# Attention in a pre-LN block: two row maxima per vector instruction, one ring of banks, a new order of steps

## The chip, the core and the metric

The kernel runs on one core of a Trainium2 chip. The metric is the device time of one execution in microseconds (us). Engines are called by the profile's names: PE (matmul), PEld (weight load), DVE (VectorE), ACT (ScalarE), POOL (GpSimd) and SP (the engine that issues most DMAs). "L228" is line 228 of the kernel.

## The reference

One block with 2048 tokens of width 512: layer norm, attention with 32 heads of 16, a residual; then layer norm and a gated MLP, and a second residual.

```python
def _A_ref(x, wqkv, wo):
    B, S, D = x.shape            # 1, 2048, 512
    H = 32; Dh = D // H          # 16
    qkv = (x @ wqkv).reshape(B, S, 3, H, Dh).transpose(2, 0, 3, 1, 4)
    q, k, v = qkv[0], qkv[1], qkv[2]
    scores = jnp.einsum("bhqd,bhkd->bhqk", q, k) * Dh ** -0.5
    p = _softmax(scores, axis=-1)
    o = jnp.einsum("bhqk,bhkd->bhqd", p, v)
    return o.transpose(0, 2, 1, 3).reshape(B, S, D) @ wo

h = x + _A_ref(_layernorm(x), wqkv, wo)
h2 = h + _B_ref(_layernorm(h), w_in, w_sp, b_sp, w_out)   # the gated MLP, not touched here
```

The softmax subtracts a maximum of each row of scores. So the kernel needs, for each head and query, a maximum over the 2048 keys before it can take exponentials.

## The kernel before

The kernel has three parts. First come layer norm and the projections to q, k and v, then attention, then the output projection and the MLP. The change is in attention, whose instruction order is written out by hand for all engines: an engine runs its instructions in the order of the program, and tiles bring the waits between engines.

**Units and pairs.** Heads are taken four at a time (`hg`, 8 groups) and queries 512 at a time (`qb`, 4 blocks). Such a block has 16 key blocks of 128 keys. One key block is a unit, and the loop at L1045 takes two units, a pair: 256 pairs, eight in each block. Two heads (`p`) times two row halves of PE (`t`) make a group's four heads: `t` = 0 uses PE rows from 0, `t` = 1 rows from 64, so that two matmuls with 48 or 50 rows each can stand in the array side by side.

**A pair's scores.** `score` (L808) makes one 128 x 512 tile of scores in PSUM, in a bank of its own, by one matmul (`product`, L805), and ACT takes its exponential into `pt` (L814). The steps are named s0 to s7: s0 to s3 belong to the first key block, s4 to s7 to the second; odd ones have `t` = 1.

**Weighing.** `weigh` (L825) multiplies the exponentials with the values into one bank `pv`, with four column groups of PE (L830). In the order it is "P" for the pair's first key block (the whole width, 512 queries), and "H", twice, for the second key block of the pair before (256 queries each). "P" needs s0 to s3, "H" needs s4 to s7 of the pair before. At the end of a block "out" (`take`, L840) copies `pv` out on DVE and sends it to memory. The next block's "P" reuses the bank and waits for that copy.

**A pair's maxima.** Beside its scores each pair does a part of the row maxima for a later block (`max_pair`, L205): for 128 queries and two heads. With `t` = 1 it takes four maxima over 512 keys each (M0, M4, M5, M7). With `t` = 0 it takes two such (M1, M2), and for the other 1024 keys a pair of tiles: "minus" (M3, ACT takes the absolute value, L233) and "plus" (M6, a DVE instruction that combines the two, L237). A single maximum is one matmul (L223) and one DVE reduction of 128 x 512 to 128 x 1 (L228). After eight pairs one block's maxima are complete. Then `finish` ("join") reduces them to one number for each head and query (L242, DVE), and POOL scales it and splits it in two halves (L245, L246, L247). `max_rows` ("turn") transposes these on DVE (L259) and sends them over a scratch tensor into two extra rows of the query tile (L260, L263), where the score matmul adds them in. The set of maxima is made ahead: eleven pairs' worth (LEAD) is done before attention begins, so the last ten or so pairs have none.

**PSUM in attention.** There are eight banks. Scores have three in turn (`ps_s`), maxima four in turn (three of `ps_m` and `ps_m3`), and `pv` one. A matmul into a bank waits until the reader of that bank's former contents is done.

**The order.** The string PAIR (L40) gives the order of a pair's steps, and the loop at L1099 issues them:

```python
PAIR = "s0 M0 join s2 M4 M1 s1 H s3 invert M2 s5 M3 H out M5 s4 M7 turn s6 s7 M6 P".split()
```

"join" runs `finish` of the pair before, if it was the last of a block's eight. "invert" takes the reciprocal of a block's row sums (L777) in one pair of eight, after a DMA that has gathered them. POOL has other work beside, queued at the start of a pair by `work` (L1048): it scales and splits the weights of the later parts. In the pair that follows a block's last maxima no such work is queued. In the last ten pairs, which have no maxima, `scores2` (L816) makes two score tiles at a time.

Of the kernel before, what the change touches and what calls it, by code (L numbers as in the profile page):

```python
# [8 lines left out]
F32 = mybir.dt.float32  # L9
# [6 lines left out]
AX = mybir.AxisListType  # L16
PSUM = bass.MemoryType.PSUM
DRAM = bass.MemoryType.DRAM

P = 128  # L20
S = 2048
D = 512
H = 32
# [4 lines left out]
NB = S // P  # L28
# [4 lines left out]
KS = 48  # L33
# [3 lines left out]
FIRST = 2  # L37
RG = 64
VW = DH + 1
PAIR = "s0 M0 join s2 M4 M1 s1 H s3 invert M2 s5 M3 H out M5 s4 M7 turn s6 s7 M6 P".split()  # L40
HF = 3 * P
FC = FH // 2
LOW = -3.0e38
# [16 lines left out]
def block_kernel(ctx: ExitStack, tc: tile.TileContext, x, wqkv, wo, w_in, w_sp4, b_sp, w_out, out):  # L60
# [139 lines left out]
    def bank(i):  # L200
        if i in more:
            return more[i]()
        return ps_m.tile([P, 512], F32, name=f"m{i}")

    def max_pair(m):  # L205

        g, i = divmod(m, 8)
        hg, qb = divmod(g, NQ)
        q, k, w = qst[g], kst[hg % 2], uvs[hg % 2]
        if i == 0:
            mx[g] = sm.tile([P, 16, 4], F32, name="mx")
            nc.gpsimd.memset(mx[g][:, :8, 3:], LOW)
        c, p = slice(i % 4 * P, i % 4 * P + P), i // 4
        at = lambda t, e: mx[g][:, t * 8 + i, e:e + 1]

        def scores(t, keys, b):  # L220
            r = slice(RG * t, RG * t + KS)
            acc = bank(b)
            nc.tensor.matmul(acc, q[r, p, c], keys[r, p], start=True, stop=True)  # L223
            return acc

        def one(t, e, b):
            acc = scores(t, k[:, :, 512 * e:512 * e + 512], b)
            nc.vector.reduce_max(at(t, e if t else e - 1), acc, axis=AX.X)  # L228

        def minus(b):  # L230
            acc = scores(0, w[:, :, 512:], b)
            ab[0] = sm.tile([P, 512], F32, name="ab")
            nc.scalar.activation(ab[0], acc, AF.Abs)  # L233

        def plus(b):
            acc = scores(0, w[:, :, :512], b)
            nc.vector.tensor_tensor_reduce(ab[0], acc, ab[0], 0.5, LOW, ALU.add, ALU.max, at(0, 0))  # L237

        def finish():
            if i == 7:  # L240
                nm = sm.tile([P, 2, 8], F32, name="nm")
                nc.vector.tensor_reduce(nm.rearrange("p t i -> p (t i)"), mx.pop(g), axis=AX.X,  # L242
                                        op=ALU.max, negate=True)
                parts = sm.tile([P, 2, 2, 8], F16, name="mparts")
                nc.gpsimd.tensor_scalar(nm, nm, 1.0 / ONE, 1.0, op0=ALU.mult, op1=ALU.mult)  # L245
                nc.gpsimd.tensor_copy(parts[:, :, 0], nm)  # L246
                nc.gpsimd.tensor_sub(parts[:, :, 1], nm, parts[:, :, 0])  # L247
                turned[0] = (g, parts)

        ab = {}  # L250
        four = [lambda b, e=e: one(1, e, b) for e in range(4)]
        two = [lambda b, e=e: one(0, e, b) for e in (2, 3)]
        return [four[0], two[0], two[1], minus, four[1], four[2], plus, four[3], finish]

    def max_rows():

        g, parts = turned.pop(0)
        t = sm.tile([P, 32], F16, name="mturned")
        nc.vector.transpose(t, parts.rearrange("p t j i -> p (t j i)"))  # L259
        nc.sync.dma_start(m_scr[g % 2], t)  # L260
        for j in range(2):
            r0 = RG * j + KS
            nc.sync.dma_start(  # L263
                qst[g][r0:r0 + 2].rearrange("r p (c n s) -> r (p c) n s", n=4, s=32),
                m_scr[g % 2].rearrange("(n j r q) s -> j r q n s", n=4, j=2, r=2)[j])
# [476 lines left out]
    def make_h(sb, acc):  # L742

        o2, h = o2s.pop(sb), xrs[sb]
        for d in range(DB):
            for i, (a, b) in enumerate(((0, 0), (0, 1), (1, 0))):
                nc.tensor.matmul(acc, o2[a][:, d, :], wo2[b][:, d, :],
                                 start=not (d or i), stop=d == DB - 1 and i == 2)
                if d < DB - 1 or i < 2:
                    yield  # L750
        nc.vector.scalar_tensor_tensor(h, acc, h_down, h, op0=ALU.mult, op1=ALU.add)
        nc.sync.dma_start(h_scr[sb * P:(sb + 1) * P, :], h)
        hst[sb] = e2.tile([P, 6], F32, name="st")
        nc.vector.bn_stats(hst[sb], h)
# [18 lines left out]
    def invert():  # L773

        hg, cols, sums, pool = sums_.pop(0)
        rc = pool.tile([P, 16], F32, name="rcp")
        nc.vector.reciprocal(rc, sums)  # L777
        to = four_heads(r_scr.rearrange("(d h) s -> d h s", h=8), hg)[:, :, cols]
        for t in range(2):
            nc.sync.dma_start(to[t].rearrange("p (r c) -> p r c", c=16), rc[64 * t:64 * t + 64])  # L780
# [7 lines left out]
    with ExitStack() as at:  # L788
# [3 lines left out]
        fixed(kst[1])  # L792
        pp = at.enter_context(tc.tile_pool(name="pp", bufs=6))
        ps_v = at.enter_context(tc.tile_pool(name="ps_v", bufs=1, space=PSUM))
        inner = at.enter_context(ExitStack())
        ps_m3 = inner.enter_context(tc.tile_pool(name="ps_m3", bufs=1, space=PSUM))
        ps_s = inner.enter_context(tc.tile_pool(name="ps_s", bufs=3, space=PSUM))
        more.clear()
        more[3] = lambda: ps_m3.tile([P, 512], F32, name="m3")
        pv = {}  # L800

        def product(s, hg, qb, kb, p, t):
# [5 lines left out]
        def score(hg, qb, kb, p, t):  # L808

            if (p, kb) not in pts:  # L810
                pts[p, kb] = pp.tile([P, 2, 512], F32, name="pt")
            s = ps_s.tile([P, 512], F32, name="s")
            product(s, hg, qb, kb, p, t)
            nc.scalar.activation(pts[p, kb][:, t, :], s, AF.Exp, scale=scales_[hg // 2])  # L814

        def scores2(hg, qb, kb, p):  # L816

            pts[p, kb] = pp.tile([P, 2, 512], F32, name="pt")
            turn[0] += 1
            s = later[turn[0] % 3 != 1].tile([P, 2, 512], F32, name="s2")  # L820
            for t in range(2):
                product(s[:, t, :], hg, qb, kb, p, t)
            nc.scalar.activation(pts[p, kb], s, AF.Exp, scale=scales_[hg // 2])
# [221 lines left out]
        for n in range(0, len(units), 2):  # L1045
# [12 lines left out]
                copy_v()  # L1058
            if kb == 2 and n // NB + 3 < HG * NQ:
                load_q(n // NB + 3)  # L1060
            steps = max_pair(m) if m < 8 * HG * NQ else []
            m += 1
            if not steps and not later:
                maxima.close()
                later.append(attn.enter_context(
                    tc.tile_pool(name="ps_l", bufs=1, space=PSUM, side="right")))
                steps_h.append(make_h(h_rows[0], later[0].tile([P, 512], F32, name="h")))
            elif not steps and len(later) == 1:
                inner.close()
                later.append(at.enter_context(tc.tile_pool(name="ps_t", bufs=2, space=PSUM)))  # L1070
            ends = kb == 0 and n

            def join():
                if joins:
                    joins.pop()()
# [20 lines left out]
                some_h(1)  # L1096
                weigh(hg, qb, kb)
            first = True
            for tok in PAIR if len(later) < 2 else ():  # L1099
                i = int(tok[-1]) if tok[-1].isdigit() else 0  # L1100
                if tok[0] == "s":
                    score(hg, qb, (kb, kb1)[i // 4], i % 4 // 2, i % 2)
                elif tok[0] == "M" and steps:
                    steps[i](count[0] % 4)
                    count[0] += 1
                    if i == 6:
                        joins.append(steps[8])
                elif tok == "join":
                    join()
                elif tok == "H" and prev is None:  # L1110
                    if first:
                        pv[0] = ps_v.tile([P, 512], F32, name="pv")
                        for j in range(4):
                            nc.tensor.matmul(pv[0][32 * j:32 * j + 32, :], vst[0][:, :32],
                                             vst[0][:, :512], start=True, stop=True)
                    first = False
                elif tok == "H":
                    a = 0 if first else 256
                    weigh(*prev, a, a + 256)
                    first = False  # L1120
                elif tok == "P":
                    weigh(hg, qb, kb)
                elif tok == "out" and ends:
                    take(*prev[:2])
                elif tok == "invert" and kb == 6 and n > NB:
                    invert()
                elif tok == "turn" and turned:
                    max_rows()
            prev = (hg, qb, kb1)
            if len(later) == 2 and kb == 6:  # L1130
                invert()
# [472 lines left out]
```

## Time and profile before

| | |
|---|---|
| median of 3 runs | 1713.44 us (1712.44 to 1714.61) |
| span of the profiled execution | 1712.3 us, 36689 instructions |
| what lies around the span | 1.1 us, against the median |
| granted clock of PE | 1.00 in all stretches of attention |
| attention with maxima | about 161 to 1248 us |

The profiled execution is the one that the page and all answers of the trace are about. A row of a window gives, for each engine, its busy time and the count of its instructions. A row of a group gives the line, the engine, the tile written and the tiles read, the count, then after the bar the busy time and the mean duration in ns, and then the engine's idle time just before such instructions with what ended it. A row of the timeline gives the start in the span, the time to the end of the last instruction of the row, and then the instructions, merged where several of one line follow each other.

### The profile page before, as it was taken

How to read it: one execution, taken by the hardware profiler on the slowest of the kernel's cores; microseconds unless marked ns; L12 is line 12 of the kernel's file. 1: busy time of each engine (PE TensorE's matmuls, PEld its weight loads, DVE VectorE, ACT ScalarE, POOL GpSimd, SP SyncE). 2: the span in 40 equal slices, each digit the busy share in tenths (PEclk: the TensorE clock that was granted, in tenths of full speed). 3: DMA queues.
4: the chain of work that ended last, by engine and by line, in shares of the span. 5: the costliest groups of instructions: out<-in, count | busy, mean ns of one | idle time of the engine just before them, and what ended most of it. 6: DMA issues, size and time to landing. Idle time of an engine off the chain costs nothing.

```text
span 1712.3 us, 36689 instructions
## 1 busy us (share of the span) xinstructions
PE 1699.5 (99%) x13508; PEld 644.7 (38%) x13508; DVE 1452.5 (85%) x3051; ACT 1317.5 (77%) x2584; POOL 813.6 (48%) x1062
## 2 busy tenths in 40 slices
PE   9999999999999999999999999999999999999999
PEld 4533222222222222222222222222225666656665
DVE  7688999999999999999999999999936787543444
ACT  4334999999999999999999999999995545211111
POOL 1231867776673267687767776400002766300100
PEclk9999999999999999999999999999999999999999
DMA  5534332342221244344434444300114454664551
GB/s 185 167 94 144 103 89 68 101 94 82 81 68 25 56 118 117 104 144 125 130 113 124 132 140 130 80 13 19 37 39 124 140 173 140 233 234 156 198 217 44
DMA packets 189309, 196.03 MB, mean 114 GB/s; under 512 B 67496, under 2 KB 140008, under 8 KB 189128
## 3 DMA queue, kind: packets, MB, share of 16 engines
q1 hardware_dynamic: 186824, 188.04, 36.8%
q10 hardware_dynamic: 2304, 5.64, 0.8%
q8 instruction: 106, 1.74, 0.4%
q14 instruction: 75, 0.61, 0.1%
HBM read 122.10 MB, written 65.93 MB: 110 GB/s over the span
## 4 chain that ended last, share of the span: by engine, by line
PE 78%; DVE 12%; DMA 3%; POOL 2%; ACT 2%; SPq 2%; issue 1%; ACTq 0%; POOLq 0%; DVEq 0%
PE pv L830 26%; PE s L805 17%; PE m L223 9%; DVE mx L228 7%; PE acc L107 4%; PE g L108 4%; PE g L109 4%; PE g L107 4%; PE acc L109 4%; PE acc L108 4%; DMA rc<-r_scr 1%; DVE ab L237 1%; DVE og L840 1%; SPq L723 1%; DVE rs_t L124 1%
## 5 line engine op out<-in xcount | busy, mean ns | idle before, releaser
L814 ACT ACTIVATE pt<-s 128x512 f32<-128x512 f32 x1968 | 1006.2, 637 | 5.5 <-PE m L223 4.3
L228 DVE TENSOR_REDUCE mx<-m 128x1 f32<-128x512 f32 x1510 | 947.5, 682 | 11.7 <-PE m L223 2.9
L805 PE MATMUL s<-qst,kst 50*128 50x512 f16 x2048 | 604.2, 379 | 0.2
L830 PE MATMUL pv<-pt,vst 128*32 128x256 f32 (+1 forms) x6056 | 598.1, 466 | 4.1 <-DVE og L840 1.3
L223 PE MATMUL m<-kst,qst 48*128 48x512 f16 x1510 | 452.4, 381 | 0.0
L805 PEld LDWEIGHTS <-kst 50*128 50x128 f16 x2048 | 132.0, 94 | 352.1 <-issue 323.7
L830 PEld LDWEIGHTS pv<-pt,vst 128*32 128x32 f32 x6056 | 119.5, 108 | 290.7 <-issue 277.3
L223 PEld LDWEIGHTS <-qst 48*128 48x128 f16 x2048 | 159.2, 93 | 173.6 <-issue 124.2
L223 PE MATMUL m<-uvs,qst 48*128 48x512 f16 x504 | 190.5, 380 | 0.6 <-DVE mx L228 0.6
L245 POOL TENSOR_SCALAR nm<-nm 128x16 f32<-128x16 f32 x32 | 6.6, 206 | 358.8 <-DVE nm L242 358.8
L237 DVE CUSTOM_DVE_ANT_0 ab<-m,ab 128x512 f32<-128x512 f32 x252 | 170.5, 677 | 2.7 <-ACT ab L233 2.7
L233 ACT ACTIVATE ab<-m 128x512 f32<-128x512 f32 x252 | 157.3, 624 | 15.5 <-PE m L223 14.8
L1368 ACT ACTIVATE pr<-pr,up 128x304 f32<-128x304 f32 (+1 forms) x32 | 17.0, 574 | 109.2 <-DVE up L1322 109.2
L991 POOL TENSOR_TENSOR op<-raw,op 128x512 f16<-128x512 f32 x80 | 92.9, 1161 | 6.0
L914 POOL TENSOR_TENSOR raw<-raw 128x512 f32<-128x512 f32 (+1 forms) x84 | 83.3, 991 | 6.7
L919 POOL TENSOR_TENSOR acc_sp<-acc_sp,raw 128x512 f32<-128x512 f32 x63 | 80.4, 1277 | 4.5
L109 PE MATMUL acc<-wi,hT 128*128 128x344 f16 x256 | 79.1, 309 | 0.3 <-DVE hT L104 0.3
L107 PE MATMUL acc<-wi,hT 128*128 128x344 f16 x256 | 79.1, 309 | 0.0
L108 PE MATMUL acc<-wi,hT 128*128 128x344 f16 x256 | 79.1, 309 | 0.0
L1510 POOL TENSOR_TENSOR pr<-pr,z 128x344 f32<-128x344 f32 x8 | 7.3, 914 | 145.9 <-DMA whole<-squares 108.3
L911 POOL TENSOR_SCALAR raw<-raw 128x512 f32<-128x512 f32 (+1 forms) x88 | 52.3, 594 | 19.7 <-DMA raw<-in_wqkv 12.4
L1509 DVE TENSOR_TENSOR pr<-g,v 128x344 f32<-128x344 f32 x8 | 4.1, 517 | 66.6 <-PE g L109 63.5
(247 smaller groups left out, 2292.9 us busy)
## 6 DMA issues: line engine op xcount, KB each, us to landing
raw<-in_w_sp SPq DMA_DIRECT2D x128, 256.0 KB
s_scr<-op SPq DMA_DIRECT2D x64, 256.0 KB
op<-s_scr SPq DMA_DIRECT2D x32, 512.0 KB
a_scr<-op SPq DMA_DIRECT2D x48, 256.0 KB
op<-a_scr SPq DMA_DIRECT2D x24, 512.0 KB
o_scr<-og SPq DMA_DIRECT2D x64, 128.0 KB
qst<-q_scr SPq DMA_DIRECT2D x192, 32.0 KB
kst<-k_scr SPq DMA_DIRECT2D x48, 128.0 KB
```

The source lines that it names most:

```text
L107: nc.tensor.matmul(ps, lh, rh, start=first, stop=False, **kw)
L108: nc.tensor.matmul(ps, lh, rl, start=False, stop=False, **kw)
L109: nc.tensor.matmul(ps, ll, rh, start=False, stop=last, **kw)
L223: nc.tensor.matmul(acc, q[r, p, c], keys[r, p], start=True, stop=True)
L228: nc.vector.reduce_max(at(t, e if t else e - 1), acc, axis=AX.X)
L233: nc.scalar.activation(ab[0], acc, AF.Abs)
L237: nc.vector.tensor_tensor_reduce(ab[0], acc, ab[0], 0.5, LOW, ALU.add, ALU.max, at(0, 0))
L805: nc.tensor.matmul(s, kst[hg % 2][r, p, kb * P:(kb + 1) * P], qst[hg * NQ + qb][r, p, :], start=True, stop=True)
L814: nc.scalar.activation(pts[p, kb][:, t, :], s, AF.Exp, scale=scales_[hg // 2])
L830: nc.tensor.matmul(pv[0][32 * j:32 * j + 32, a:b], vst[hg % 2][:, c:c + 32], pts[j % 2, kb][:, j // 2, a:b], start=kb == 0, stop=kb == NB - 1,
L914: pool.tensor_mul(got[0] if n else acc, got[0], got[0])
L991: chores.append((lambda: pool.tensor_sub(t[0][:, 1], of(), t[0][:, 0]), TT))
```

## The change

Four of the six single maxima of a pair become two double ones. `both` writes two matmuls (one with `t` = 0, one with `t` = 1) into the two banks of a tile `dd`, and one DVE instruction reduces 128 x 2 x 512 to two columns of the maxima's tile. There is one such tile, so the second double of a pair waits for the first one's reduction. All other tiles of a pair (eight scores, two single maxima, minus and plus) take turns in one ring of five banks, whoever reads them. With `pv` that makes eight banks again.

The order of steps is new. In it "X" is a double maximum, "N" a single one, "A" is minus, "C" is plus, "Q" is what "H" was, "R" what "P" was, and "rows" stands for join and invert. The first pair of a block has an order of its own, with "out" and without "rows". `plus` now comes behind the whole product R, and "turn" two tokens behind "rows". In the pairs without maxima, the tile `dd` and four newly opened banks serve `scores2`, and the tile `h` for the output projection is made when the ring has closed.

```diff
-PAIR = "s0 M0 join s2 M4 M1 s1 H s3 invert M2 s5 M3 H out M5 s4 M7 turn s6 s7 M6 P".split()
+PAIR = "s1 X s3 s4 Q s0 N s2 s5 Q X A N s6 rows s7 turn R C".split()
+FIRST_PAIR = "s1 X s3 s4 Q N s0 s2 Q out s5 X A s7 s6 N turn R C".split()
+SINGLES = 5
...
+    class Banks:
+
+        def __init__(self, pools, double):
+            self.pools = [pool for pool, n in pools for _ in range(n)]
+            self.turn, self.double = 0, double
+
+        def one(self):
+            i = self.turn % len(self.pools)
+            self.turn += 1
+            return self.pools[i].tile([P, 512], F32, name=f"c{i}")
+
+        def two(self):
+            return self.double.tile([P, 2, 512], F32, name="dd")
...
-            acc = bank(b)
+            acc = banks.one() if banks else bank(b)
...
+        def both(e):
+            acc = banks.two()
+            for t in range(2):
+                keys = k[:, :, 512 * (e - 2 * t):512 * (e - 2 * t) + 512]
+                r = slice(RG * t, RG * t + KS)
+                nc.tensor.matmul(acc[:, t, :], q[r, p, c], keys[r, p], start=True, stop=True)
+            a = 4 * i + e - 1
+            nc.vector.reduce_max(mx[g].rearrange("p n e -> p (n e)")[:, a:a + 32:31], acc, axis=AX.X)
...
+        if banks:
+            wide = PAIR.count("X")
+            return {"N": four[wide:], "n": two[wide:], "A": [minus], "C": [plus], "end": finish,
+                    "X": [lambda e=e: both(e) for e in (2, 3)]}
...
+        maxima.close()
+        more.clear()
+        ps_d = at.enter_context(tc.tile_pool(name="ps_d", bufs=1, space=PSUM))
         inner = at.enter_context(ExitStack())
-        ps_m3 = inner.enter_context(tc.tile_pool(name="ps_m3", bufs=1, space=PSUM))
-        ps_s = inner.enter_context(tc.tile_pool(name="ps_s", bufs=3, space=PSUM))
-        more.clear()
-        more[3] = lambda: ps_m3.tile([P, 512], F32, name="m3")
+        ps_c = inner.enter_context(tc.tile_pool(name="ps_c", bufs=1, space=PSUM))
+        banks = Banks([(ps_c, SINGLES)], ps_d)
...
-            s = ps_s.tile([P, 512], F32, name="s")
+            s = banks.one()
...
-            s = later[turn[0] % 3 != 1].tile([P, 2, 512], F32, name="s2")
+            s = banks.two() if turn[0] % 3 == 1 and SINGLES == 5 else later[1].tile([P, 2, 512], F32, name="s2")
...
-            steps = max_pair(m) if m < 8 * HG * NQ else []
+            steps = max_pair(m, banks) if m < 8 * HG * NQ else []
             m += 1
             if not steps and not later:
-                maxima.close()
-                later.append(attn.enter_context(
-                    tc.tile_pool(name="ps_l", bufs=1, space=PSUM, side="right")))
-                steps_h.append(make_h(h_rows[0], later[0].tile([P, 512], F32, name="h")))
+                later.append(None)
             elif not steps and len(later) == 1:
                 inner.close()
+                later[0] = at.enter_context(tc.tile_pool(name="ps_l", bufs=1, space=PSUM))
                 later.append(at.enter_context(tc.tile_pool(name="ps_t", bufs=2, space=PSUM)))
+                steps_h.append(make_h(h_rows[0], later[0].tile([P, 512], F32, name="h")))
...
-            for tok in PAIR if len(later) < 2 else ():
+            for tok in (FIRST_PAIR if ends else PAIR) if len(later) < 2 else ():
...
+                elif tok in ("A", "C", "N", "n", "X"):
+                    if steps:
+                        steps[tok].pop(0)()
...
+                elif tok == "R":
                     weigh(hg, qb, kb)
-                elif tok == "out" and ends:
+                elif tok == "out":
                     take(*prev[:2])
-                elif tok == "invert" and kb == 6 and n > NB:
-                    invert()
+                elif tok == "rows":
+                    join()
+                    if kb == 6 and n > NB:
+                        invert()
                 elif tok == "turn" and turned:
                     max_rows()
+            if steps:
+                joins.append(steps["end"])
             prev = (hg, qb, kb1)
```

More of the change, by code (lines that the diff above doesn't have):

```diff
@@ L203, in bank, with max_pair @@
         return ps_m.tile([P, 512], F32, name=f"m{i}")
-    def max_pair(m):
+    class Banks:
[8 more added lines that the diff above has]
+            return self.double.tile([P, 2, 512], F32, name="dd")
+    def max_pair(m, banks=None):
         g, i = divmod(m, 8)
@@ L221, in scores, with one, minus @@
             r = slice(RG * t, RG * t + KS)
-            acc = bank(b)
+            acc = banks.one() if banks else bank(b)
             nc.tensor.matmul(acc, q[r, p, c], keys[r, p], start=True, stop=True)
             return acc
-        def one(t, e, b):
+        def one(t, e, b=None):
             acc = scores(t, k[:, :, 512 * e:512 * e + 512], b)
             nc.vector.reduce_max(at(t, e if t else e - 1), acc, axis=AX.X)
-        def minus(b):
+        def both(e):
[6 more added lines that the diff above has]
+            nc.vector.reduce_max(mx[g].rearrange("p n e -> p (n e)")[:, a:a + 32:31], acc, axis=AX.X)
+        def minus(b=None):
             acc = scores(0, w[:, :, 512:], b)
@@ L233, in minus, with plus @@
             nc.scalar.activation(ab[0], acc, AF.Abs)
-        def plus(b):
+        def plus(b=None):
             acc = scores(0, w[:, :, :512], b)
@@ L250, in max_pair @@
         ab = {}
-        four = [lambda b, e=e: one(1, e, b) for e in range(4)]
-        two = [lambda b, e=e: one(0, e, b) for e in (2, 3)]
+        four = [lambda b=None, e=e: one(1, e, b) for e in range(4)]
+        two = [lambda b=None, e=e: one(0, e, b) for e in (2, 3)]
+        if banks:
+            wide = PAIR.count("X")
+            return {"N": four[wide:], "n": two[wide:], "A": [minus], "C": [plus], "end": finish,
+                    "X": [lambda e=e: both(e) for e in (2, 3)]}
         return [four[0], two[0], two[1], minus, four[1], four[2], plus, four[3], finish]
@@ L1098, in block_kernel @@
             first = True
-            for tok in PAIR if len(later) < 2 else ():
-                i = int(tok[-1]) if tok[-1].isdigit() else 0
+            for tok in (FIRST_PAIR if ends else PAIR) if len(later) < 2 else ():
                 if tok[0] == "s":
+                    i = int(tok[1])
                     score(hg, qb, (kb, kb1)[i // 4], i % 4 // 2, i % 2)
[L1103 to L1110, printed above, removed]
+                elif tok in ("A", "C", "N", "n", "X"):
+                    if steps:
+                        steps[tok].pop(0)()
+                elif tok == "Q" and prev is None:
                     if first:
@@ L1116, in block_kernel @@
                     first = False
-                elif tok == "H":
+                elif tok == "Q":
                     a = 0 if first else 256
@@ L1120, in block_kernel @@
                     first = False
-                elif tok == "P":
+                elif tok == "R":
                     weigh(hg, qb, kb)
-                elif tok == "out" and ends:
+                elif tok == "out":
                     take(*prev[:2])
-                elif tok == "invert" and kb == 6 and n > NB:
-                    invert()
+                elif tok == "rows":
+                    join()
+                    if kb == 6 and n > NB:
+                        invert()
                 elif tok == "turn" and turned:
                     max_rows()
+            if steps:
+                joins.append(steps["end"])
             prev = (hg, qb, kb1)
```

## The prediction

> **What bounds the kernel now.** First the page's busy line, then the windows of a stretch of attention, then the groups of 200 to 1250 us.
>
> ```profile
> PE 1699.5 (99%) x13508; PEld 644.7 (38%) x13508; DVE 1452.5 (85%) x3051; ACT 1317.5 (77%) x2584; POOL 813.6 (48%) x1062
> 600.00:700.00 100.00, 99.66 (x904) 28.19 (x905) 99.25 (x194) 99.95 (x205) 72.66 (x104) 1.00 0.40 112
> L814 ACT ACTIVATE pt<-s 128x512 f32<-128x512 f32 x1892 | 967.5, 637 | 2.1 <-PE m L223 1.0
> L228 DVE TENSOR_REDUCE mx<-m 128x1 f32<-128x512 f32 x1418 | 888.9, 682 | 7.6
> ```
>
> In attention PE, DVE and ACT are all over 99% busy, so busy time can't say which of them sets the pace. The timelines can. Of ACT, with one L233 row in each pair of key blocks:
>
> ```profile
> 656.94 0.62 ACT L233 ACTIVATE ab<-m 128x512 f32<-128x512 f32 x1
> 661.35 0.62 ACT L233 ACTIVATE ab<-m 128x512 f32<-128x512 f32 x1
> 665.86 0.64 ACT L233 ACTIVATE ab<-m 128x512 f32<-128x512 f32 x1
> 670.36 0.64 ACT L233 ACTIVATE ab<-m 128x512 f32<-128x512 f32 x1
> 674.79 0.62 ACT L233 ACTIVATE ab<-m 128x512 f32<-128x512 f32 x1
> 675.27 4.06 ACT L814 ACTIVATE pt<-s 128x512 f32<-128x512 f32 x8
> 679.20 0.62 ACT L233 ACTIVATE ab<-m 128x512 f32<-128x512 f32 x1
> ```
>
> A plain pair lasts 4.41 us (674.79 to 679.20) and holds nine ACT instructions: 0.49 each. They overlap (0.62 long, the next one 0.48 later), and the eight end at 679.33, 0.49 before the end of the ninth (679.82): no gap. **ACT is saturated.** Now PE:
>
> ```profile
> 672.52 0.37 PE L805 MATMUL s<-qst,kst 50*128 50x512 f16 x1
> 672.82 0.64 PE L830 MATMUL pv<-pt,vst 128*32 128x256 f32 x8
> 673.39 0.39 PE L805 MATMUL s<-qst,kst 50*128 50x512 f16 x1
> 673.40 0.39 PE L223 MATMUL m<-kst,qst 48*128 48x512 f16 x1
> 673.62 0.38 PE L805 MATMUL s<-qst,kst 50*128 50x512 f16 x1
> 673.93 0.64 PE L830 MATMUL pv<-pt,vst 128*32 128x256 f32 x8
> 674.50 0.39 PE L223 MATMUL m<-kst,qst 48*128 48x512 f16 x1
> 674.73 0.38 PE L223 MATMUL m<-kst,qst 48*128 48x512 f16 x1
> 675.29 1.06 PE L830 MATMUL pv<-pt,vst 128*32 128x512 f32 x8
> 676.29 0.39 PE L805 MATMUL s<-qst,kst 50*128 50x512 f16 x1
> ```
>
> A score and a maximum on opposite row halves start together (673.39, 673.40): one slot of 0.23 us. From the last slot of a group to a product it is 0.30 (672.52 to 672.82, 673.62 to 673.93); a half product takes 0.57, a whole one 1.00. Eight slots in groups of three, two and three with their products need 5 x 0.23 + 3 x 0.30 + 2 x 0.57 + 1.00 = 4.19. DVE:
>
> ```profile
> 699.79 3.07 DVE L228 TENSOR_REDUCE mx<-m 128x1 f32<-128x512 f32 x5
> L1357 DVE TENSOR_REDUCE low<-pr 128x2 f32<-128x768 f32 x7 | 6.7, 953 | 0.7
> ```
>
> Five reductions of 0.68 in 3.07 make one per (3.07 - 0.68) / 4 = 0.60, so seven vector steps are 4.2 in a pair. So PE and DVE have about 0.2 us of slack per pair and ACT has none. Between 200 and 1250 us, 1892 exponentials and 237 absolutes at 0.49 make 1043 of the 1050 us. Only 7 us are not ACT's own.
>
> **What the change does, part by part.** *ACT*: eight exponentials and one absolute per pair as before, so 4.41 stays the floor, and whatever DVE saves is not on the path. At most those 7 us and their like can come back.
>
> *Double maxima.* From the rows 768 columns cost 0.953 and 512 cost 0.682: 1.06 ns a column. A reduction over 1024 then lasts 0.682 + 0.54 = 1.22, and one follows after 0.60 + 0.54 = 1.14. Two of them save 4 x 0.60 - 2 x 1.14 = 0.12 us per pair on DVE, under ACT's cover. The end that saves nothing (1.20) leaves DVE at its old load, so the pair is still 4.41; there is no end at which the saving shows.
>
> The Trainium skill, "VectorE: DVE Perf Modes", section "The DRAIN you can't avoid", has the next instruction start only when the pipe is empty, and its rules for kernel authors say to minimise the number of operations. By that, two singles would be 1.36 and a double 1.22, 0.28 saved per pair. The trace has the next reduction start 0.08 before the former's end, so the measurement decides; the full saving is a rival below.
>
> *The ring of five and the new order.* PE now runs [C of the pair before, s1, X, s3, s4] Q [s0 N s2 s5] Q [X A N s6 s7] R: again eight slots, 4.19. But a step now waits for the bank used five single steps earlier, whichever engine reads it. The remaining durations:
>
> ```profile
> 748.22 0.39 PE L805 MATMUL s<-qst,kst 50*128 50x512 f16 x1
> 748.65 2.56 ACT L814 ACTIVATE pt<-s 128x512 f32<-128x512 f32 x5 [0.78 <-PE m L223]
> L814 ACT ACTIVATE pt<-s x1968: 591/645/680, 160.7 to 1253.5; 128x512 f32<-128x512 f32 x197
> 661.30 0.68 DVE L840 COPY og<-pv 128x512 f32<-128x512 f32 x1
> 662.04 1.06 PE L830 MATMUL pv<-pt,vst 128*32 128x512 f32 x8
> ```
>
> From a matmul's start its reader starts 0.43 later (748.22 to 748.65), and an exponential ends 1.02 after it (0.43 + 0.59). A reader's end frees PE 0.05 later (661.98 to 662.04). Put 0 at the end of s1's exponential. With ACT saturated the others end at s3 0.49, s4 0.98, s0 1.47, s2 1.96, s5 2.45, A 2.94, s6 3.43, s7 3.92, next s1 4.41. Each matmul must start 1.02 before its end.
>
> - s2 takes s1's bank (from 0.05), s5 takes s3's (0.54), A s4's, N s0's, s7 s2's (2.01), C s5's, the next s1 A's.
> - s5 starts at 0.54, Q at 0.84, X at 1.41, A and N at 1.64, s6 at 1.85, s7 at 2.01, R at 2.31. C and the next s1 start at 3.31 and end at 4.33: **0.08 early**.
> - then X at 3.54 and s3, s4 at 3.76; Q at 4.06 and s0 at 4.63, ending 5.65 against 5.88.
> - DVE, in the same clock: C 3.74, X 4.34, N 5.48, the next X at 6.25 (it waits for PE), N 7.39 to 8.07. That N frees the following s3, whose matmul must start by 8.29: 0.17 early.
>
> So a plain pair should stay at 4.41, at small margins.
>
> *First pair of a block.* Before, DVE's copy og holds R: R started at 662.04 instead of 0.30 after its last slot, and the ACT rows above show 4.51, 4.50 and 4.43 for three pairs: 0.21 us lost per block. In the new order og starts on DVE at 1.66, ends 2.34, and R starts at 2.39 instead of 2.31: inside the 0.08. The loss should go: 30 blocks x 0.21 = 6.3 us. Its other end is nothing gained.
>
> *`rows` and `turn`.* Once per eight pairs `rows` issues L242 on DVE, POOL makes three small steps, and `turn` issues L259, which waits for POOL:
>
> ```profile
> 681.77 0.21 DVE L242 TENSOR_REDUCE nm<-mx 128x16 f32<-128x64 f32 x1
> 682.07 0.20 POOL L245 TENSOR_SCALAR nm<-nm 128x16 f32<-128x16 f32 x1 [6.67 <-DVE nm L242]
> 682.62 0.22 POOL L247 TENSOR_TENSOR mparts<-nm,mparts 128x16 f16<-128x16 f32 x1
> 684.95 0.20 DVE L259 STREAM_TRANSPOSE mturned<-mparts 128x32 f16<-128x32 f16 x1
> 685.08 0.65 DVE L237 CUSTOM_DVE_ANT_0 ab<-m,ab 128x512 f32<-128x512 f32 x1
> ```
>
> POOL stands idle for L242 and is done 1.07 us after its start (682.84). Before, five reductions stood between the two DVE steps (681.77 to 684.95), so nothing waited. Now only s7 stands between `rows` and `turn`, and s7 gives DVE nothing: **DVE waits for POOL**. In the clock above L242 follows N at 3.58, L259 can start at 3.58 + 1.07 + 0.05 = 4.70, and C, queued behind it, at 4.82 instead of 3.74. C ends at 5.50 and X follows at 5.43. PE's N sits in front of s2 and s5 and wants C's bank: 5.55 instead of 4.63. The next N on DVE starts at 4.82 + 0.61 + 1.14 = 6.57 and ends 7.25; s6 takes its bank at 7.30, then R 7.60, s1 8.60, its exponential 9.62 instead of 8.82. **0.80 us lost**; after it every step is back at its place behind ACT. How near a row comes:
>
> ```profile
> 746.07 0.25 DVE L777 RECIPROCAL rcp<-sums 128x16 f32<-128x16 f32 x1 [0.86 <-DMA sums<-o_scr]
> 745.78 0.62 ACT L233 ACTIVATE ab<-m 128x512 f32<-128x512 f32 x1
> 751.05 0.64 ACT L233 ACTIVATE ab<-m 128x512 f32<-128x512 f32 x1
> ```
>
> There DVE stood still for 0.86, and that pair took 5.27: 0.86 too long. The bounds for the new wait are 0 (the slack of the ring takes it up) and 1.08 (all of it lands on ACT). I take 0.80, by the layout and near that row. It occurs where a pair with vector steps follows the last of eight maxima: 30 times, 24.0 us. Moving L777 behind the last N gives its DMA some 2 us more, so the one 0.86 goes. L260's write on SP's queue comes about 1.5 us later in its pair, with three pairs before its data are used.
>
> *Start and end.* Eleven sets of maxima come before attention, and ten pairs without maxima after it; they keep their instructions, and the pools only change places: 0, within 1 us.
>
> **Sum:** 24.0 - 6.3 - 0.9 = +16.8 us on a span of 1712.3, so 1729.1. The median of the runs lies 1.1 above the span: about **1730 us**. With the wait at 0.5 to 1.08 (15 to 32 us) and the copy at 0 to 6.3, the forecast's own range is 1720 to 1745.
>
> **Rivals.**
> 1. *The wait is taken up* (faster). If PE and ACT have enough work in hand to cross DVE's stop, only the copy's 6.3 and the 0.9 count: 1706. For it: DVE carries 0.12 us per pair less. Against: the ring is shared, so N's wait for C holds s2 and s5 in PE's queue, and the 0.86 above was not taken up. It holds if s6 gets its bank by 6.50 in that clock instead of 7.30, so that s1 starts by 7.80. 0.14.
> 2. *The vector saving counts in full* (faster): 0.12 x 245 = 29 us, 1684; 0.28 by the page. Against: ACT's rows without a gap. 0.02.
> 3. *Plain pairs get longer* (slower by more). The margin at s1 is 0.08; if a double or a bank's release is 0.18 later than laid out, each pair gains 0.1 or so: 245 x 0.1 = 24 on top, 1754. For it: every release sits on one ring. Against: the layout closes at 4.41. 0.16.
> 4. *The halves cancel*: half of the wait lands (0.3) and the copy's gain is whole: 9.0 - 7.2, 1715. 0.08.
>
> **How the numbers follow.** Forecast 0.60. A difference of 0.2% (3.4 us) is about what can be told from no change. Faster 0.14 + 0.02 = 0.16, same 0.08, slower 0.60 + 0.16 = 0.76. The range 1710 to 1752 holds the forecast, most of rival 4 and half of rival 3; it leaves out rivals 1 and 2 and the other half, 2 in 10.
>
> **What would show it.** ACT's L233 rows should be 4.41 us apart in plain pairs; a larger step says rival 3. Around each L242 one or two steps should sum to 0.8 too much, with L259 idle before it until POOL L247, some 30 times, about 30 us of DVE idle in all (0.98 each). If the idle is there and the L233 steps are not longer, rival 1 holds. At the og copies the three steps should be 4.41. The double reductions should last 1.22. What would make it wrong: PE not pairing the two halves of X in one slot, or POOL reaching L245 late.

## The result and the profile after

The changed kernel takes 1737.3 us (median of four runs, 1736.88 to 1737.56), the kernel before 1713.8 beside it. The ratio is 1.0139, with a 95% interval of 1.0126 to 1.0151: slower by 23.5 us. The profiled spans, 1735.6 and 1712.3, differ by 23.3.

The page's busy line, a window and a group of the changed kernel, against those shown of before:

```profile
PE 1710.6 (99%) x13508; PEld 633.3 (36%) x13508; DVE 1431.2 (82%) x2561; ACT 1325.4 (76%) x2584; POOL 811.8 (47%) x1062
600.00:700.00 100.00, 98.27 (x881) 26.46 (x873) 94.98 (x145) 98.39 (x200) 64.72 (x99) 1.00 0.41 108
L253 DVE TENSOR_REDUCE mx<-dd 128x2 f32<-128x1024 f32 x490 | 599.0, 1222 | 0.2 <-PE dd L251 0.2
```

DVE works 21 us less than before (1431.2 for 1452.5), and a double reduction lasts 1.222 us, as worked out. But ACT, busy for 98.39 us of the window where it was 99.95, does 200 instructions where it did 205. So the vector engine became cheaper and ACT now has gaps. ACT's timeline says where. Of the changed kernel, one row per pair, over eight pairs:

```profile
655.49 0.71 ACT L258 ACTIVATE ab<-c 128x512 f32<-128x512 f32 x1
659.90 0.70 ACT L258 ACTIVATE ab<-c 128x512 f32<-128x512 f32 x1
664.99 0.60 ACT L258 ACTIVATE ab<-c 128x512 f32<-128x512 f32 x1 [0.23 <-PE c L239]
669.61 0.66 ACT L258 ACTIVATE ab<-c 128x512 f32<-128x512 f32 x1
673.99 0.69 ACT L258 ACTIVATE ab<-c 128x512 f32<-128x512 f32 x1
678.59 0.66 ACT L258 ACTIVATE ab<-c 128x512 f32<-128x512 f32 x1
682.98 0.68 ACT L258 ACTIVATE ab<-c 128x512 f32<-128x512 f32 x1
687.37 0.70 ACT L258 ACTIVATE ab<-c 128x512 f32<-128x512 f32 x1
```

The steps are 4.41, then 5.09, 4.62 and 4.38, then 4.60, 4.39 and 4.39. A plain pair has kept its 4.41. Two places of a block are longer: one by 5.09 + 4.62 + 4.38 - 3 x 4.41 = 0.86, the other by 4.60 + 4.39 + 4.39 - 3 x 4.41 = 0.15, where it was 0.21 before. DVE's timeline and PE's at the first place:

```profile
657.10 0.69 DVE L262 CUSTOM_DVE_ANT_0 ab<-c,ab 128x512 f32<-128x512 f32 x1 [0.17 <-PE c L835]
661.25 0.21 DVE L267 TENSOR_REDUCE nm<-mx 128x16 f32<-128x64 f32 x1
662.36 0.21 DVE L288 STREAM_TRANSPOSE mturned<-mparts 128x32 f16<-128x32 f16 x1 [0.90 <-POOL mparts L272]
662.49 0.67 DVE L262 CUSTOM_DVE_ANT_0 ab<-c,ab 128x512 f32<-128x512 f32 x1
```

```profile
662.30 0.39 PE L835 MATMUL c<-qst,kst 50*128 50x512 f16 x1
663.23 0.37 PE L239 MATMUL c<-kst,qst 48*128 48x512 f16 x1 [0.54 <-DVE mx L262]
663.23 0.58 PE L835 MATMUL c<-qst,kst 50*128 50x512 f16 x2
```

L267 is the small reduction of `rows`, L288 the transpose of `turn`, L262 `plus`. DVE stands still for 0.90 us until POOL is done; `plus` queues behind it; PE's single maximum (663.23) waits for the bank of `plus`; and the scores s2 and s5 queue behind that matmul. The groups of the whole of attention count it up: DVE's idle time before L288 is 25.9 us in 29 times (a thirtieth lies ahead of that window).

```profile
L288 DVE STREAM_TRANSPOSE mturned<-mparts 128x32 f16<-128x32 f16 x29 | 6.1, 212 | 25.9 <-POOL mparts L272 23.2 <-POOL mx L232 2.7
```

30 blocks x 0.86 make 25.8 us, and the steps of all 30 blocks sum to 26.0. The other place gives back less than the rows above promise: 19 of the 30 blocks have the 0.15, but every fourth has 0.24 or more and single ones up to 0.52 (why, no run here shows), so that all 30 sum to 5.9 us where they summed to 6.3 before. The wait of L777 is gone, which gives 0.8 back. So from the first absolute value of attention to the last it takes 24.8 us more (165.0 to 1273.5, before 164.3 to 1248.0). What lies around it is 1.5 us shorter, and the spans differ by 23.3. The theory to test: DVE's wait for POOL goes through the banks to ACT. Its rival: the new order and the shared ring make those pairs long, and the wait merely falls into them.

### The profile page after: what moved, and what is told of

Read it like the earlier page. It is cut to its first block, busy times and chain, and to the rows that moved or that the text cites. A ratio compares the mean times of both kernels' runs of the same rounds, so it can differ in the third digit from the quotient of the medians.

```text
span 1735.6 us, 36903 instructions
## 1 busy us (share of the span) xinstructions
PE 1710.6 (99%) x13508; PEld 633.3 (36%) x13508; DVE 1431.2 (82%) x2561; ACT 1325.4 (76%) x2584; POOL 811.8 (47%) x1062
## 4 chain that ended last, share of the span: by engine, by line
PE 77%; DVE 12%; DMA 3%; issue 3%; ACT 2%; POOL 2%; SPq 2%; ACTq 0%; DVEq 0%; POOLq 0%
PE pv L860 25%; PE c L835 13%; PE c L239 8%; PE dd L251 6%; PE acc L109 4%; PE g L110 4%; PE g L111 4%; PE g L109 4%; DVE mx L253 4%; PE acc L111 4%; PE acc L110 4%; DVE ab L262 3%; DVE mx L244 2%; DMA rc<-r_scr 1%; SPq L752 1%
## 5 line engine op out<-in xcount | busy, mean ns | idle before, releaser
L844 ACT ACTIVATE pt<-c 128x512 f32<-128x512 f32 x1968 | 1022.1, 654 | 15.4 <-PE c L835 8.0
L253 DVE TENSOR_REDUCE mx<-dd 128x2 f32<-128x1024 f32 x490 | 599.0, 1222 | 0.2 <-PE dd L251 0.2
L835 PE MATMUL c<-qst,kst 50*128 50x512 f16 x1968 | 478.0, 379 | 0.0
L244 DVE TENSOR_REDUCE mx<-c 128x1 f32<-128x512 f32 x490 | 333.9, 681 | 0.5 <-PE c L239 0.5
L239 PE MATMUL c<-kst,qst 48*128 48x512 f16 x490 | 186.2, 380 | 16.0 <-DVE mx L262 16.0
L251 PE MATMUL dd<-kst,qst 48*128 48x512 f16 x980 | 195.4, 381 | 0.7 <-DVE mx L253 0.3
L262 DVE CUSTOM_DVE_ANT_0 ab<-c,ab 128x512 f32<-128x512 f32 x245 | 168.8, 689 | 28.7 <-PE c L835 28.0
L239 PE MATMUL c<-uvs,qst 48*128 48x512 f16 x490 | 186.6, 381 | 0.0
L258 ACT ACTIVATE ab<-c 128x512 f32<-128x512 f32 x245 | 165.0, 673 | 7.1 <-PE c L239 7.1
L239 PEld LDWEIGHTS <-qst 48*128 48x128 f16 x1068 | 75.3, 94 | 227.3 <-issue 226.7
L251 PEld LDWEIGHTS <-qst 48*128 48x128 f16 x980 | 52.5, 94 | 89.5 <-issue 88.1
```

The source lines that it names most:

```text
L251: nc.tensor.matmul(acc[:, t, :], q[r, p, c], keys[r, p], start=True, stop=True)
L253: nc.vector.reduce_max(mx[g].rearrange("p n e -> p (n e)")[:, a:a + 32:31], acc, axis=AX.X)
L835: nc.tensor.matmul(s, kst[hg % 2][r, p, kb * P:(kb + 1) * P], qst[hg * NQ + qb][r, p, :], start=True, stop=True)
```

## Experiments

Times are medians. The kernel before took 1713.15, 1713.18 and 1713.34 us beside the three groups of runs.

### The wait taken away from its end, and from its beginning

```diff
-PAIR = "s1 X s3 s4 Q s0 N s2 s5 Q X A N s6 rows s7 turn R C".split()
+PAIR = "s1 X turn s3 s4 Q s0 N s2 s5 Q X A N s6 rows s7 R C".split()        # e1
+PAIR = "s1 X join s3 s4 Q s0 N s2 s5 Q X A N s6 rows s7 turn R C".split()   # e2
```

In e2 "join" runs `finish`, and "rows" keeps only the reciprocal.

> The changed kernel, but `turn` is issued behind the next pair's first double maximum instead of two tokens behind `rows`, so that vector work stands between L267 and the transpose. Theory (DVE's wait for POOL costs ACT 0.86 us per block): 30 x 0.86 = 25.8 us less than 1737.3, so 1711.5, and the idle time before the transpose goes from 24.9 us to under 2. Rival (the new order and the shared ring themselves make the long pairs, the wait only falls into them): no change, 1735 to 1739, with the 5.08 us steps still there.

> The changed kernel, but `join` is issued behind the pair's first double maximum (the reciprocal stays where `rows` was, and `turn` stays at its place), so that POOL has about 3 us for its three small steps. Theory: the same 25.8 us come back, 1711.5, though this moves the other end of the wait than the experiment before. Rival (order and ring): no change, 1735 to 1739.

Measured: e1 1711.78, e2 1711.97. The group of the transpose in attention, of e1:

```profile
L288 DVE STREAM_TRANSPOSE mturned<-mparts 128x32 f16<-128x32 f16 x29 | 5.8, 201 | 0.0
```

No idle time is left before the transpose, and 25.5 us are gone. Order, ring and double maxima are all still there. Moving either end of the wait does the same, so it is the wait and not the place of one step. The rival falls.

### The wait put into the kernel before

```diff
-PAIR = "s0 M0 join s2 M4 M1 s1 H s3 invert M2 s5 M3 H out M5 s4 M7 turn s6 s7 M6 P".split()
+PAIR = "s0 M0 join turn s2 M4 M1 s1 H s3 invert M2 s5 M3 H out M5 s4 M7 s6 s7 M6 P".split()
```

> The kernel before, with one edit: `turn` directly behind `join`, so that DVE waits for POOL there too. It adds the suspected cost alone to the old order and the old separate rings. Theory (a stop of 1 us on DVE goes through to ACT whatever the rings): by the 0.86 us row of the trace of before 30 x 0.8 = 24 us, 1738; at least 10 us, since DVE has under 0.1 us of slack per pair there. Rival (only the shared ring of five carries the wait to ACT; the four banks of the maxima take it up): under 5 us more, 1713 to 1719.

Measured: 1743.79, ratio 1.0177 (1.0160 to 1.0194), 30.6 us more. DVE's timeline and ACT's there:

```profile
697.69 0.21 DVE L259 STREAM_TRANSPOSE mturned<-mparts 128x32 f16<-128x32 f16 x1 [0.90 <-POOL mparts L247]
```

```profile
694.02 0.62 ACT L233 ACTIVATE ab<-m 128x512 f32<-128x512 f32 x1
698.43 0.62 ACT L233 ACTIVATE ab<-m 128x512 f32<-128x512 f32 x1
703.85 0.64 ACT L233 ACTIVATE ab<-m 128x512 f32<-128x512 f32 x1
```

The same 0.90 us of idle time, and a step of 5.42, 1.01 too long: all of the wait goes to ACT, and a little more. One moved token, in the old order with its separate rings, costs more than the whole change did. So the wait needs no shared ring to reach ACT, and the new arrangement loses less by it (0.86).

### Half the wait

```diff
-PAIR = "s1 X s3 s4 Q s0 N s2 s5 Q X A N s6 rows s7 turn R C".split()
+PAIR = "s1 X s3 s4 Q s0 N s2 s5 Q X A rows N s6 s7 turn R C".split()
```

> The changed kernel with `rows` one step earlier, in front of the single maximum N, so that N's reduction covers 0.6 us of POOL's work and DVE stands still for about 0.4 us instead of 0.9. Theory (the ring takes up the first part of a stop, then each ns goes to ACT; C at 4.22 in the clock of the prediction, free of loss up to 3.96): 0.26 us per block, 30 x 0.26 = 8 us over e2, 1719 to 1721. Rival 1 (loss in proportion to the wait): 0.38, 1723 to 1725. Rival 2 (a stop this short is taken up): 1711 to 1713.

Measured: 1719.28, ratio 1.0037 (1.0023 to 1.0051): 7.3 us over e2, or 0.24 in each of 30 blocks. The group:

```profile
L288 DVE STREAM_TRANSPOSE mturned<-mparts 128x32 f16<-128x32 f16 x29 | 6.1, 211 | 8.7 <-POOL mparts L272 8.7
```

The idle time is 8.7 / 29 = 0.30 per block, a little less than the 0.4 of the layout, since one reduction now stands between the two steps. The time is the theory's (1719 to 1721). With idle 0.90 and loss 0.86 beside it, loss and idle run nearly side by side, with 0.05 or so free; by this measured idle a loss in proportion would be 0.29, 1720.7, so this run does not tell a small free part from proportion. A stop this short being taken up is excluded.

### What the double maxima are worth

e4 makes each double two singles again and gives their tile's two banks to the ring; e6 keeps tile and ring and only reduces each half by an instruction of its own.

```diff
-SINGLES = 5
+SINGLES = 7
-PAIR = "s1 X join s3 s4 Q s0 N s2 s5 Q X A N s6 rows s7 turn R C".split()
+PAIR = "s1 n N join s3 s4 Q s0 N s2 s5 Q n N A N s6 rows s7 turn R C".split()
...
-            a = 4 * i + e - 1
-            nc.vector.reduce_max(mx[g].rearrange("p n e -> p (n e)")[:, a:a + 32:31], acc, axis=AX.X)
+            nc.vector.reduce_max(at(0, e - 1), acc[:, 0, :], axis=AX.X)      # e6
+            nc.vector.reduce_max(at(1, e - 2), acc[:, 1, :], axis=AX.X)
```

> The kernel of e2, but each double maximum as two singles, and the tile of two banks given to the ring (seven banks for all). DVE then has 0.12 us more per pair. Theory (ACT sets the pair, the doubles save nothing on the path): within 6 us of e2, 1708 to 1718. Rival (the vector saving counts in full): 0.12 x 245 = 29 us above e2, about 1740.

> The kernel of e2 with the double tile and the ring as they are, but each double tile reduced by two instructions of 512 columns. Only DVE's load changes, by 0.12 us per pair. Theory (the load lies under ACT in this ring; in e4 the ring of seven, where s5 waits for a single maximum's bank, was what cost): up to 5 us above e2, 1712 to 1717. Rival (the saved vector time is on the path in this order): 29 us above e2, about 1741.

Measured: e4 1747.08, 35 us above e2, over the rival's figure; e6 1721.52, 9.6 us above e2. DVE's load per pair is the same in both, so most of e4's loss isn't that load. PE's timeline and DVE's of a plain pair of e4 show the rest:

```profile
645.74 0.39 PE L239 MATMUL c<-uvs,qst 48*128 48x512 f16 x1
647.47 0.53 PE L835 MATMUL c<-qst,kst 50*128 50x512 f16 x2
650.25 0.39 PE L239 MATMUL c<-uvs,qst 48*128 48x512 f16 x1
```

```profile
646.27 0.69 DVE L262 CUSTOM_DVE_ANT_0 ab<-c,ab 128x512 f32<-128x512 f32 x1
646.89 1.88 DVE L244 TENSOR_REDUCE mx<-c 128x1 f32<-128x512 f32 x3
```

The pair lasts 4.51 (645.74 to 650.25). In a ring of seven, s5 takes the bank of the pair's first single maximum. Its matmul is the second in the row at 647.47 and ends at 648.00 with the row; the row is 0.53 long where a single matmul is 0.39, so it started 0.15 late, at about 647.63. The first of the three reductions behind `plus` ends at 646.89 + 0.68 = 647.57. So scores wait for a vector step that waits for `plus`, which waits for PE: a loop through PE and DVE of 4.51. The ring's length sets who waits for whom, not only how long.

In e6 the 9.6 us are the saved vector time that the forecast had put under cover. Of e6, ACT's timeline from a block's first pair on, and then from the pair with `join` on:

```profile
666.22 0.62 ACT L258 ACTIVATE ab<-c 128x512 f32<-128x512 f32 x1
670.85 0.66 ACT L258 ACTIVATE ab<-c 128x512 f32<-128x512 f32 x1
675.38 0.64 ACT L258 ACTIVATE ab<-c 128x512 f32<-128x512 f32 x1
679.78 0.65 ACT L258 ACTIVATE ab<-c 128x512 f32<-128x512 f32 x1
688.59 0.66 ACT L258 ACTIVATE ab<-c 128x512 f32<-128x512 f32 x1
693.12 0.64 ACT L258 ACTIVATE ab<-c 128x512 f32<-128x512 f32 x1
697.52 0.65 ACT L258 ACTIVATE ab<-c 128x512 f32<-128x512 f32 x1
701.97 0.62 ACT L258 ACTIVATE ab<-c 128x512 f32<-128x512 f32 x1
```

The steps are 4.63, 4.53 and 4.40: 0.33 too long behind the copy, where the changed kernel has 0.15. At `join` they are 4.53, 4.40 and 4.45, 0.15 too long, where e2 has 4.46, 4.37 and 4.43, 0.03 too long. The plain pairs stay at 4.40 to 4.41. So the saving shows at the two places of a block where DVE has more instructions than usual: 30 x (0.18 + 0.12) = 9.0 of the 9.6 us.

### Is ACT the bound of a plain pair?

```diff
         def minus(b=None):
             acc = scores(0, w[:, :, 512:], b)
+            if banks:
+                ab[0] = still
+                return
             ab[0] = sm.tile([P, 512], F32, name="ab")
             nc.scalar.activation(ab[0], acc, AF.Abs)
```

> The kernel of e2 without ACT's absolute value in attention (`plus` combines with a tile of zeros; the matmul of `minus` stays), so the row maxima lack that part. ACT has eight instructions of 0.49 in a pair, 3.92. Theory (ACT sets the plain pair; next comes the loop s2's release, s7, R, s1, which the layout puts at 4.33): 245 x 0.08 = 20 us under e2, 1690 to 1697. Rival (PE or DVE sets the plain pair already): no change, 1709 to 1713.

Measured: 1713.15. With a ninth of ACT's work gone, nothing is gained. ACT's timeline and PE's in a pair of e5:

```profile
650.97 4.03 ACT L849 ACTIVATE pt<-c 128x512 f32<-128x512 f32 x8 [0.36 <-PE c L840]
655.39 1.08 ACT L849 ACTIVATE pt<-c 128x512 f32<-128x512 f32 x2 [0.41 <-PE c L840]
```

```profile
650.45 0.39 PE L840 MATMUL c<-qst,kst 50*128 50x512 f16 x1
653.42 0.53 PE L840 MATMUL c<-qst,kst 50*128 50x512 f16 x2
653.87 1.07 PE L865 MATMUL pv<-pt,vst 128*32 128x512 f32 x8
654.88 0.39 PE L840 MATMUL c<-qst,kst 50*128 50x512 f16 x1
```

ACT now idles 0.36 to 0.41 us per pair, and the pair still lasts 4.43 (650.45 to 654.88). It waits for s1: s7 takes s2's bank, R follows s7, s1 follows R. The layout had this loop at 4.33 with 0.43 from a matmul to its reader; for s1 the rows show 650.45 to 650.97, 0.52. So the loop is as long as ACT's nine instructions: in the new order ACT is full, and right behind it stands a loop of PE, ACT and the ring that would give the same pair.

### The first pair of a block

In e7 the last pair of a block ends "... X A s7 s6 C R N" and the next one starts with s0. In e9 the copy of `pv` is cut to 32 columns.

```diff
-FIRST_PAIR = "s1 X s3 s4 Q N s0 s2 Q out s5 X A s7 s6 N turn R C".split()
+FIRST_PAIR = "s0 X s3 s4 Q N s2 s1 Q out s5 X A s7 s6 N turn R C".split()   # e7
+LAST_PAIR = "s1 X s3 s4 Q s0 N s2 s5 Q X A s7 s6 C R N".split()
...
-            o = pool.tile([P, 512], F32, name="og", bufs=2)
-            nc.vector.tensor_copy(o, pv[0])
+            o = blank
+            nc.vector.tensor_copy(o[:, :32], pv[0][:, :32])                  # e9
```

> The kernel of e2 with an order of its own for the last pair of a block: `plus` goes in front of R and a single maximum behind it, and the next block's first pair starts with s0 in place of s1. DVE then begins the first pair with a reduction, not with `plus`, about 0.1 us earlier, and so ends the copy of pv earlier. Theory (the first pair is long because `plus` starts 0.53 after its matmul where 0.43 was laid out, and the copy then holds R): of the 0.17 us per block 0.10 to 0.17 go, 30 x that = 3 to 5 us, 1707 to 1709. Rival (something else makes the first pair long): 1711 to 1713.

> The kernel of e2 with the copy of pv at a block's end cut from 512 to 32 columns (the rest of what is sent is a constant, so most of attention's result is left out); DVE's copy then takes about 0.1 us in place of 0.6 and nothing else changes. Theory (the first pair of a block is 0.17 us too long because R waits for the copy): 30 x 0.17 = 5 us under e2, 1706 to 1708, and the 4.60 us steps go to 4.43 or less. Rival (the first pair is long because of its own order, with nine slots of PE in place of eight): 1711 to 1713.

Measured: e7 1711.74, no gain: the rival's figure. But the total does not decide here. In e7's trace the first pair is no longer long: the absolutes at 657.43, 662.05 and 666.46 are 4.62 and 4.41 apart. The long step now lies one pair earlier, at the new last pair, whose own order costs as much.

e9 took 1721.4, and its total can't be read either: in the last stage PE stood still for 10.2 us in one piece, until the maxima of a loaded weight were there, and that load was issued at 1459.27 where e2 issues it at 1449.59. Why it was late is not shown. A window of e9, and then the same of e2:

```profile
1460.00:1480.00 20.00, 9.95 (x59) 6.49 (x60) 11.03 (x24) 4.26 (x8) 2.42 (x4) 0.74 0.98 357
```

```profile
1460.00:1480.00 20.00, 20.00 (x141) 13.52 (x139) 12.85 (x34) 6.87 (x12) 6.28 (x8) 1.00 0.74 280
```

Attention itself can be read. The lines' own views give the first and the last of ACT's absolutes, of e2 and then of e9:

```profile
L258 ACT ACTIVATE ab<-c x245: 597/703/707, 165.0 to 1248.5; 128x512 f32<-128x512 f32 x123
```

```profile
L260 ACT ACTIVATE ab<-c x245: 598/699/702, 164.6 to 1245.0; 128x512 f32<-128x512 f32 x123
660.87 0.69 ACT L260 ACTIVATE ab<-c 128x512 f32<-128x512 f32 x1
665.39 0.65 ACT L260 ACTIVATE ab<-c 128x512 f32<-128x512 f32 x1
669.75 0.70 ACT L260 ACTIVATE ab<-c 128x512 f32<-128x512 f32 x1
```

1083.5 us have become 1080.4, and the first pair's steps are 4.52, 4.36 and 4.41 where e2 has 4.60, 4.39 and 4.39: 0.06 too long in place of 0.15. So about half of the first pair's excess is the copy. DVE's rows and PE's of that first pair of e9 show what else holds R:

```profile
659.80 0.68 DVE L246 TENSOR_REDUCE mx<-c 128x1 f32<-128x512 f32 x1
660.40 0.18 DVE L872 COPY blank<-pv 128x32 f32<-128x32 f32 x1
660.53 0.39 PE L837 MATMUL c<-qst,kst 50*128 50x512 f16 x2
660.75 0.38 PE L241 MATMUL c<-kst,qst 48*128 48x512 f16 x1
661.05 1.07 PE L862 MATMUL pv<-pt,vst 128*32 128x512 f32 x8
```

The short copy is over at 660.58, and R starts 0.30 behind its last slot, so the copy no longer holds it. That last slot, a single maximum, stands behind s7 and s6 (660.53), which start 0.05 after the reduction of the pair's other single maximum ends (659.80 + 0.68 = 660.48): in the first pair's order s7 takes that maximum's bank. In the changed kernel it is the same (the reduction ends at 673.61, s7 starts at 673.66), and R then waits for the copy besides (674.21 and 674.26). So DVE holds R twice, and this pair has nine slots of PE in place of eight. What the ninth slot alone costs was not tried.

### The repaired change against the kernel before

e10 is e1 once more.

> The kernel of e1 again, with more rounds, to say whether the repaired change is ahead of the kernel before at all. By the steps of ACT's absolute values a block of eight pairs takes 35.44 us there and 35.49 before: 30 x 0.05 = 1.5 us, so a ratio of 0.9991.

Measured: 1711.76, ratio 0.9991 (0.9982 to 1.0000). The repaired change is 1.6 us ahead by the medians, and the interval reaches to no difference at all: it is level with the kernel before. No other kernel here is further ahead.

## Why the prediction was right, and where it was not

- **The wait of `turn`** was the main term, 30 x 0.80 = 24.0 us. Measured 0.86 per block, and e1 and e2 gave back 25.5 and 25.3. The layout's path (L288 late, `plus` behind it, PE's single maximum waiting for its bank, scores behind that) is the one in the rows. The idle time was 0.90 where 0.98 was forecast.
- **Plain pairs** at 4.41: right. But the idle 0.17 before `plus` is more than the layout has (0.08: N ends at 8.07 - 4.41 = 3.66, `plus` starts at 3.74). `plus` starts 0.53 after its matmul (666.28 to 666.81) where 0.43 was laid out. Plain pairs kept their 4.41 all the same.
- **"The loss should go" at the first pair of a block** failed: 6.3 us were expected back, and in most blocks 0.21 became only 0.15; over all 30 blocks 0.3 us came. This is the largest part of the error of 6.5 us (23.3 between the spans, 16.8 forecast); the wait adds 2.0, and 1.5 that came back around attention was forecast as nothing. The step took R's earliest start, 2.31, from the order of a plain pair. The first pair has another order, with a ninth slot and with s7 waiting for a reduction, and that was not laid out. The margin of 0.08 was also less than the 0.10 by which `plus`, and DVE's queue behind it, ran late. By e9 the copy is about half of what remained.
- **The one 0.86** went as forecast: L777 has no such wait in the changed kernel.
- **"There is no end at which the saving shows"** was wrong in part. e6 without the saving is 9.6 us slower. In the plain pairs ACT covers DVE; behind a copy and at `join` it doesn't. The price of it in the sum was nothing, since the change has the saving.
- **"ACT has none"**, of slack, holds, but "so 4.41 stays the floor" left out that the new order's own loop is just as long. The layout had 4.33 for it; e5 showed 4.43.
- **The rivals.** The wait was not taken up (rival 1: e8, even 0.30 us were not). The vector saving in full (rival 2, with the rule of the Trainium skill's page "VectorE: DVE Perf Modes", section "Rules for kernel authors", on the number of operations) did not come: DVE's busy time fell by 21 us and the kernel got slower; e6 prices the saving at 9.6 us, a third of 29. The section "The DRAIN you can't avoid" of the same page of the Trainium skill, by which the prediction worked out 0.28, also says that an operation that is not held starts earlier; the rows at the end of this document, 0.60 apart at 0.68 long, agree with that. Plain pairs did not get longer (rival 3), and more than half of the wait landed (rival 4). The wait and the copy both erred to the same side, and only the 1.5 around attention to the other, so little of the total's nearness is luck.

## What to carry to other kernels

When three engines are all 99% busy, lay out one period with every release, and look first for an instruction that waits for a slow helper engine while work stands behind it. Put independent work between a small result that goes out to another engine and the step that takes it back: here one token's place was worth 25 us, and the change with that token moved is 1.6 us ahead by the medians. A smaller load on an engine pays only at the places where that engine is the late one.

## What the runs showed of the hardware

- Two maxima in one instruction save 0.06 to 0.07 us, not the 0.14 that their durations suggest (2 x 0.68 for 1.22). Starts on DVE, of the changed kernel:

```profile
641.30 0.68 DVE L244 TENSOR_REDUCE mx<-c 128x1 f32<-128x512 f32 x1
641.90 1.22 DVE L253 TENSOR_REDUCE mx<-dd 128x2 f32<-128x1024 f32 x1
643.03 0.68 DVE L244 TENSOR_REDUCE mx<-c 128x1 f32<-128x512 f32 x1
```

  The next instruction starts 0.60 after a single and 1.13 to 1.14 after a double: neighbours overlap, so what an instruction costs in a queue is the distance of starts, not its duration.
- From a matmul to the start of its reader it was 0.43 us in the row that the layout used (748.22 to 748.65). Of `plus` and s1, whose matmuls start together behind a product, one reader came later: in the changed kernel `plus` started 0.53 after its matmul (666.28 to 666.81) and s1's exponential 0.45 (666.28 to 666.74), in e5 `plus` 0.42 (650.44 to 650.87) and s1's 0.52. What decides which is late is not shown.
- Three tiny POOL steps on 128 x 16 elements, with both hand-overs, keep DVE waiting for 0.90 us, longer than the reduction of a single maximum lasts (0.68).
